# Longer packets, fewer fillers and earlier ranks at the head of an attention and mixture-of-experts kernel

## The chip, the cores and the metric

The kernel runs on one core of a Trainium2 chip. The metric is the device time of one execution in microseconds, the median of several runs.

## The reference

Linear attention is followed by two layers that send each token to one of eight experts. Cut to what matters:

```python
kv = np.einsum('bhsd,bhse->bhde', k, v)            # 4 batches, 8 heads, 576 rows, 64 wide
out = np.einsum('bhsd,bhde->bhse', q, kv)
x = out / np.sqrt(np.mean(out * out, -1, keepdims=True) + 1e-06) * g_norm   # to 2304 x 512

# first layer: a token with x @ w_skip > 0 goes to its best expert, the others stay as they are
e_idx = np.argmax(xc @ w_gate, axis=1)
h = np.maximum(xc[mask] @ w1[e], 0.0)               # 512 -> 1024
y[mask] = gate_w[mask, None] * (h @ w2[e])          # 1024 -> 512
out[do_compute] = xc + y

# second layer: every token, at most `capacity` per expert (576), the rest get 0
out[i] = gate_w[i] * y[expert_idx[i], pos[i]]
```

All of it is in 32-bit floating point. The order of k's and v's rows inside a batch does not change their product's sum.

## The kernel before

The kernel has three parts in one program. In the **attention part** the 2304 tokens are 18 tiles of 128 rows (`emit_tile`, L843). For each of the four batches `load_kv` (L737) and `load_q` (L753) bring k, v and q from the SyncE queue, `emit_kv` (L765) adds up the product of k and v in five steps c0 to c4 (four chunks of 128 rows and a rest of 64), and `emit_kvT` (L785) copies and transposes it and multiplies it by the gate weights. `emit_products` (L809) multiplies q by it for one tile into a bank pool of three (`apo`). ScalarE squares the tile and copies it out, VectorE takes the mean, its inverse and the logits (L850 to L863), GpSimd multiplies the copy by the gain and by the inverse (`multiply`, L827), and the rows are stored into a table in HBM, `xcat`, from the SyncE queue (L947).

TensorE's order is written out by hand. `ATT_SEQ` (L35) has one string for each batch: tN is a tile of that batch, mN its products alone, gN its gain, pN the rest of it, cN a step of the next batch's kv, T the end of that kv, r and R the two halves of `rank_part1` (L214), e and E the head of the first slot (`early1`, L871, and `early1_rows`, L878), f a run of fillers, w one load of the first slot's weights, q the transposes of its rows, h its first hidden step, s stores. The other engines' orders follow from these and from priorities.

`rank_part1` finds for the tokens seen so far which expert takes them and at what position. It runs once over tiles 0 to 8 and once over tiles 9 to 17. The first run also names the expert with most tokens; that expert's first 128 tokens are the first slot, and they are gathered from `xcat` and worked on while the attention part still runs. `As` (L271) and `Bt` are the two sides of the table of tokens, which TensorE multiplies (L883, L963). `EARLY_SEQ` (L34) is the order after the last tile: hidden steps h1 to h3, the second ranks R, output chunks y0 to y3, and T, the table.

A **filler** is a matrix product of zeros (`warm`, L109) that nothing reads. `WARM_0` (L36) has the number after each kv step of batch 0, `WARM_T` that in `emit_kvT`, `WARM_E` that of f.

In the **first layer** eight slots (one for each expert, by size) are worked in order (L1284 to L1317): two products, the tokens' new logits, and `add_tokens` (L995), which adds the slot's tokens to the table of the second layer in steps (`todo`). In slot 6 `early` (L1158) names the first expert of the second layer, gathers its rows and starts its weights. The **second layer** works its slots in the same way with every operand split in two halves. Weight buffers (`wr`) are a ring of six of 1 MB, used for k and v first.

## Time and profile before

| | us |
|---|---|
| median of three runs | 484.43 (483.7 to 484.61) |
| the profiled execution | 485.83 |
| its span, first to last instruction | 484.1 |
| TensorE busy in it | 470.4 |
| VectorE busy | 298.8 |
| ScalarE busy | 203.6 |
| GpSimd busy | 145.3 |

The profile is of one execution; times in it count from the start of its span. A row of the timeline has the start, the length, the engine, the line, the operation with what it writes and reads, how many instructions stand together, and in brackets how long the engine was idle before and what ended that. PE is TensorE, PEld its weight loads, DVE VectorE, ACT ScalarE, POOL GpSimd, SP SyncE. A matrix product in 32 bits counts as two instructions. A busy TensorE may be busy with fillers.

### The profile page before, as it was taken

How to read it: one execution, taken by the hardware profiler on the slowest of the kernel's cores; microseconds unless marked ns; L12 is line 12 of the kernel's file. 1: busy time of each engine (PE TensorE's matmuls, PEld its weight loads, DVE VectorE, ACT ScalarE, POOL GpSimd, SP SyncE). 2: the span in 40 equal slices, each digit the busy share in tenths (PEclk: the TensorE clock that was granted, in tenths of full speed). 3: DMA queues.
4: the chain of work that ended last, by engine and by line, in shares of the span. 5: the costliest groups of instructions: out<-in, count | busy, mean ns of one | idle time of the engine just before them, and what ended most of it. 6: DMA issues, size and time to landing. Idle time of an engine off the chain costs nothing.

```text
span 484.1 us, 10279 instructions
## 1 busy us (share of the span) xinstructions
PE 470.4 (97%) x3852; PEld 444.6 (92%) x3852; DVE 298.8 (62%) x950; ACT 203.6 (42%) x507; POOL 145.3 (30%) x179
## 2 busy tenths in 40 slices
PE   8999989999999999999899999999999999999995
PEld 3788788999999999999798999999999999999985
DVE  2367786676676755448694664756747656776611
ACT  1575542545353331225142553554545544555400
POOL 5586865022213113111243220401506033040201
PEclk9999999999999999999999999999999999999999
DMA  7999967997876955566039964554755566310001
GB/s 264 396 395 351 326 227 256 323 367 288 289 238 219 329 195 195 173 231 247 24 94 413 391 259 168 201 189 129 248 176 191 185 229 213 110 38 1 36 24 40
DMA packets 23641, 104.90 MB, mean 217 GB/s; under 512 B 3529, under 2 KB 3657, under 8 KB 14880
## 3 DMA queue, kind: packets, MB, share of 16 engines
q1 hardware_dynamic: 16144, 76.70, 44.6%
q0 software_dynamic: 7152, 27.40, 16.2%
q8 instruction: 32, 0.52, 0.4%
q14 instruction: 25, 0.20, 0.1%
q10 hardware_dynamic: 288, 0.07, 0.1%
HBM read 92.15 MB, written 12.76 MB: 217 GB/s over the span
## 4 chain that ended last, share of the span: by engine, by line
PE 74%; DVE 5%; DMA 3%; issue 1%; ACT 0%; POOL 0%; POOLq 0%; ACTq 0%
PE hp L677 13%; PE yp L1197 8%; PE yp L1198 8%; PE yp L1199 8%; PE hp L1197 6%; PE yp L701 6%; PE hp L1198 6%; PE hp L1199 6%; PE yp L711 3%; PE yp L702 2%; PE yt L1426 2%; PE tp L1382 2%; DMA wraw<-in_w2b 1%; DVE wlo L1087 1%; PE tp L659 1%; PE tp L1118 1%
## 5 line engine op out<-in xcount | busy, mean ns | idle before, releaser
L1086 ACT CAST whi<-wraw 128x512 fp32r<-128x512 f32 x152 | 86.3, 621 | 75.2 <-PE yp L1198 30.1
L1087 DVE TENSOR_TENSOR wlo<-wraw,whi 128x512 fp32r<-128x512 f32 x152 | 97.4, 684 | 28.9 <-ACT whi L1086 27.7
L416 POOL DMA_INDIRECT rows<-xcat,gi x40 | 42.6, 1064 | 149.0 <-ACT ex L425 87.8
L1197 PE MATMUL hp<-xh,whi 128*128 128x256 f32 (+7 forms) x256 | 78.9, 308 | 0.3 <-DVE hl L1217 0.2
L1199 PE MATMUL hp<-xh,wlo 128*128 128x256 f32 (+7 forms) x256 | 76.7, 299 | 0.0
L1198 PE MATMUL hp<-xl,whi 128*128 128x256 f32 (+7 forms) x256 | 76.6, 299 | 0.0
L677 PE MATMUL hp<-xT,wraw 128*128 128x140 f32 (+8 forms) x560 | 75.6, 291 | 0.5 <-ACT xT L661 0.5
L677 PEld LDWEIGHTS hp<-xT,wraw 128*128 128x128 f32 x560 | 71.6, 190 | 2.6 <-issue 1.8
L1197 PE MATMUL yp<-hh,whi 128*128 128x320 f32 (+5 forms) x192 | 58.8, 306 | 0.0
L1416 POOL DMA_INDIRECT out<-ot,toki x24 | 32.9, 1372 | 83.3 <-DVE su L429 39.5
L1198 PE MATMUL yp<-hl,whi 128*128 128x320 f32 (+5 forms) x192 | 57.3, 298 | 0.0
L1199 PE MATMUL yp<-hh,wlo 128*128 128x320 f32 (+5 forms) x192 | 57.3, 298 | 0.0
L1197 PEld LDWEIGHTS hp<-xh,whi 128*128 128x128 f32 x256 | 48.2, 188 | 1.0 <-DVE hl L1217 0.7
L1198 PEld LDWEIGHTS hp<-xl,whi 128*128 128x128 f32 x256 | 48.4, 189 | 0.0
L1199 PEld LDWEIGHTS hp<-xh,wlo 128*128 128x128 f32 x256 | 48.3, 189 | 0.0
L701 PE MATMUL yp<-hT,whi 128*128 128x352 f32 (+4 forms) x160 | 43.1, 351 | 0.0
L1136 POOL DMA_INDIRECT xcat<-rows,toki x16 | 17.0, 1062 | 82.4 <-DVE mxt L374 79.9
L1216 ACT ACTIVATE hh<-hp 128x320 fp32r<-128x320 f32 (+8 forms) x64 | 27.2, 430 | 32.2 <-PE hp L1199 27.4
L1217 DVE SCALAR_TENSOR_TENSOR hl<-hp,hh 128x320 fp32r<-128x320 f32 (+8 forms) x64 | 30.1, 477 | 13.7 <-ACT hh L1216 12.5
L702 PE MATMUL yp<-hT,wlo 128*128 128x176 f32 (+4 forms) x160 | 37.8, 236 | 0.0
L1198 PEld LDWEIGHTS yp<-hl,whi 128*128 128x128 f32 x192 | 36.2, 189 | 0.0
L1197 PEld LDWEIGHTS yp<-hh,whi 128*128 128x128 f32 x192 | 36.1, 188 | 0.0
(284 smaller groups left out, 854.2 us busy)
## 6 DMA issues: line engine op xcount, KB each, us to landing
wraw<-in_w2a SPq DMA_DIRECT2D x14, 1024.0 KB, 6.6
wraw<-in_w1b SPq DMA_DIRECT2D x14, 1024.0 KB
wraw<-in_w2b SPq DMA_DIRECT2D x14, 1024.0 KB, 5.2
wraw<-in_w1a SPq DMA_DIRECT2D x13, 1024.0 KB
xcat<-xa SPq DMA_DIRECT2D x18, 264.0 KB, 5.2
q<-in_q SPq DMA_DIRECT2D x4, 1152.0 KB
wraw<-in_k SPq DMA_DIRECT2D x6, 512.0 KB, 9.6
wraw<-in_v SPq DMA_DIRECT2D x6, 512.0 KB
```

What stands on the lines that cost most here:

```text
L416: return nc.gpsimd.indirect_dma_start(out=rows[:n], out_offset=None, in_=xcat[0:source], in_offset=bass.IndirectOffsetOnAxis(ap=gi[:n], ax ...
L677: nc.tensor.matmul(hp[:, ff, :], lhsT=wv[:, fc % 4, k, :], rhs=XT[j][:, k, c0:c1], start=(k == 0), stop=(k == 3))
L701: nc.tensor.matmul(yp, lhsT=wh[:, fc, :], rhs=HT[j][:, fc], start=(fc == 0), stop=False, skip_group_check=True)
L702: nc.tensor.matmul(yp[:, 0, :], lhsT=wl[:, fc, :], rhs=HT[j][:, fc, 0, :], start=False, stop=(fc == 7), skip_group_check=True)
L1086: nc.scalar.copy(out=hi[:, cs], in_=raw[:, cs])
L1087: ins = nc.vector.tensor_tensor(out=lo[:, cs], in0=raw[:, cs], in1=hi[:, cs].bitcast(F32), op=ALU.subtract)
L1197: nc.tensor.matmul(ps, lhsT=wh, rhs=xh, start=first, stop=False)
L1198: nc.tensor.matmul(ps, lhsT=wh, rhs=xl, start=False, stop=False)
L1199: nc.tensor.matmul(ps, lhsT=wl, rhs=xh, start=False, stop=last)
L1216: ea = nc.scalar.activation(out=hh[:, fs, cs], in_=hp, func=AF.Relu)
L1217: ev = nc.vector.scalar_tensor_tensor(out=hl[:, fs, cs], in0=hp, scalar=0.0, in1=hh[:, fs, cs].bitcast(F32), op0=ALU.max, op1=ALU.subtract)
L1416: st = nc.gpsimd.indirect_dma_start(out=out, out_offset=bass.IndirectOffsetOnAxis(ap=r2["toki"][:nn, j, bi:bi + 1], axis=0), in_=ot[:nn], ...
```

## The change

- k and v of a batch are loaded in two halves of two chunks, and each partition takes rows that follow one another, so that two chunks of a partition are one run of 4 KB. Batch 0 did it in four single chunks.
- There are 14 fillers at the start instead of 10, 3 instead of 15 between the kv steps of batch 0, 6 instead of 12 at f.
- The capacity is read into one partition; the overflow branch, where all 128 are wanted, reads it again.
- The first ranks stand ahead of tile 9, compare against the row of numbers in SBUF, and leave `bump` and `head` for after the table (`lead1_bump`). Tiles 9 and 10 have their products and copies early and the rest after the table; the gain is multiplied later.
- The kv of batch 3 lives in a bank of the tiles' pool, the transpose of batch 2's kv too.
- q of batch 3 is loaded after the stores of batch 1.
- The first slot's weights: the first half comes from GpSimd's queue after the gather, the other three from ScalarE's.
- VectorE multiplies tiles 12 and 14 by the gain straight from PSUM, instead of a copy by ScalarE and a product by GpSimd.
- The third hidden step of the first slot is cut in two around the second ranks, and the two bank pools there change places.
- In slot 6 of the first layer the third output chunk goes ahead of the last steps of the table, and `bump` is added after the fourth.

The core of the diff:

```diff
-G_DVE = ()
-EARLY_SEQ = "h1 x h2 R h3 y0 T y1 y2 y3"
-ATT_SEQ = ["t0 c0 c1 t1 t2 c2 c3 c4 t3 T s", "t0 t1 t2 c0 c1 t3 t4 c2 c3 c4 T s", "r c0 c1 t0 R e m1 g1 s9 w c2 c3 c4 m2 T E f p1 p2 t3", "t0 t1 s10 w s11 q t2 h0 t3 t4 s14 w s r"]
-WARM_0 = (5, 3, 5, 2, 0)
+G_DVE = (12, 14)
+EARLY_SEQ = "h1 x h2 a3 R b3 y0 T y1 y2 y3"
+ATT_SEQ = ["t0 c0 c1 t1 t2 c2 c3 c4 t3 T s", "t0 t1 t2 c0 c1 t3 t4 c2 c3 c4 T s l", "r c0 c1 R m0 g0 e m1 g1 c2 c3 c4 E T f p0 p1 w w w t2 t3", "t0 t1 s9 s10 q t2 h0 t3 s12 t4 s r"]
+WARM_0 = (0, 3, 0, 0, 0)
-WARM_E = 12
+WARM_E = 6
...
-    cap_i = cst.tile([128, 2], I32, name="cap_i")
-    nc.scalar.dma_start(out=cap_i, in_=capacity.bitcast(I32).unsqueeze(0).to_broadcast([128, 2]))
-    capf = cst.tile([128, 1], F32, name="capf")
+    cap_i = cst.tile([1, 2], I32, name="cap_i")
+    nc.scalar.dma_start(out=cap_i, in_=capacity.bitcast(I32).unsqueeze(0))
+    capf = cst.tile([1, 1], F32, name="capf")
...
-            nc.tensor.matmul(lg[:, 256:384], lhsT=ones[0:1], rhs=rowb[0:1], start=True, stop=True)
...
-            ahead["first"] = nc.vector.tensor_scalar(out=As[:, i0 + i, :], in0=row, scalar1=a[:, i:i + 1], scalar2=None, op0=ALU.is_equal)
+            ahead["first"] = nc.vector.tensor_scalar(out=As[:, i0 + i, :], in0=rowb, scalar1=a[:, i:i + 1], scalar2=None, op0=ALU.is_equal)
...
-        warm(p1u.tile([128, 512], F32, name="acc"), 10)
+        warm(p1u.tile([128, 512], F32, name="acc"), 14)
...
-            step = 1 if b == 0 else 2
-            for c in range(0, 4, step):
+            for c in range(0, 4, 2):
-                    nc.sync.dma_start(out=t[:, c:c + step, :], in_=src[b, o:o + 512].rearrange("(c p) d -> p c d", c=4)[:, c:c + step, :])
+                    nc.sync.dma_start(out=t[:, c:c + 2, :], in_=src[b, o:o + 512].rearrange("(p c) d -> p c d", c=4)[:, c:c + 2, :])
...
-            load_q(b)
+            if b < B - 1:
+                load_q(b)
...
+                if b == B - 1:
+                    spare.append(apo.tile([128, 4, 256], F32, name="ops").rearrange("p c n -> p (c n)"))
+                    kvp[b] = spare[-1][:, 0:512].rearrange("p (c n) -> p c n", c=4)
...
             if i in G_DVE:
                 nc.vector.tensor_tensor(out=og4, in0=o4, in1=grep.unsqueeze(1).unsqueeze(1).to_broadcast([128, 4, 2, HD]), op=ALU.mult)
-            else:
+                return
+            if i not in gained:
                 nc.scalar.copy(out=og4, in_=o4)
+            gained.add(i)
+            if whole:
                 multiply(og, og, grep.unsqueeze(1))
...
-                W[0].append(load_w(w1a, 1, nc.values_load(r1["lead"][0][0:1, 0:1], engines=[mybir.EngineType.Pool], min_val=0, max_val=E - 1,
-                                                          skip_runtime_bounds_check_because="the index of an expert"), nc.gpsimd, g))
+                W[0].append(load_w(w1a, 0, nc.values_load(r1["lead"][0][0:1, 0:1], engines=[mybir.EngineType.Pool], min_val=0, max_val=E - 1,
+                                                          skip_runtime_bounds_check_because="the index of an expert"), nc.gpsimd, g, ahead))
...
-                        W[0].append(load_w(w, hf, ahead["reg"], nc.sync, ahead["store"]))
+                        W[0].append(load_w(w, hf, ahead["reg"], nc.scalar))
...
             l2(j, 1)
+            if j == E - 2:
+                l2(j, 2)
             next(todo)
...
-            l2(j, 2)
+            if j != E - 2:
+                l2(j, 2)
+            l2(j, 3)
             if j == E - 2:
                 add(cnt2, identb, bump)
-            l2(j, 3)
```

## Rows read from the trace of the kernel before

**Rows 1.** The page: busy time and share, granted clock in forty slices.

```profile
PE 470.4 (97%) x3852; PEld 444.6 (92%) x3852; DVE 298.8 (62%) x950; ACT 203.6 (42%) x507; POOL 145.3 (30%) x179
...
PEclk9999999999999999999999999999999999999999
```

**Rows 2.** Waits of TensorE, 0 to 130 us: total, times, longest.

```profile
PE lg L241 <- DVE oh L167: 1.3, 1, 1.3
```

**Rows 3.** Timeline of TensorE, from the start into batch 1.

```profile
1.48 4.23 PE L112 MATMUL acc<-zb 128*128 128x512 bf16 x10 [1.48 <-DVE zb L107]
...
8.36 0.69 PE L777 MATMUL acc<-wraw 128*64 128x64 f32 x16 [0.28 <-DMA wraw<-in_v]
...
10.35 1.25 PE L112 MATMUL lg<-zb 128*128 128x512 bf16 x5
...
12.69 0.68 PE L777 MATMUL acc<-k,v 64*64 64x64 f32 x16
...
17.94 1.15 PE L777 MATMUL acc<-wraw 128*64 128x64 f32 x32
```

**Rows 4.** Timeline around the first ranks and the first gather.

```profile
39.20 0.24 DVE L159 TENSOR_REDUCE lg<-xa 128x9 f32<-128x72 f32 x1 [1.76 <-ACT kvbd L804]
...
46.79 1.10 DVE L271 TENSOR_SCALAR As<-lg,a 128x128 bf16<-128x128 f32 x4
...
48.38 2.75 PE L112 MATMUL ops<-zb 128*128 128x512 bf16 x12 [0.24 <-ACT kvbd L804]
...
49.80 1.28 POOL L416 DMA_INDIRECT rows<-xcat,gi  x1 [4.24 <-DMA xcat<-xa]
```

**Rows 5.** VectorE's groups, 40 to 66 us: count, busy us, mean ns, idle before.

```profile
L850 DVE TENSOR_REDUCE ss<-sq 128x8 f32<-128x512 f32 x9 | 6.0, 677 | 3.8 <-ACT sq L848 3.8
L863 DVE TENSOR_REDUCE xa<-lh 128x17 f32<-128x136 f32 x9 | 3.3, 377 | 0.1
...
L861 DVE TENSOR_TENSOR lh<-ops,ri 128x136 f32<-128x136 f32 x9 | 2.6, 292 | 0.2
L858 DVE RECIPROCAL ri<-rm 128x8 f32<-128x8 f32 x9 | 1.8, 199 | 0.1
L934 DVE COPY xT<-lg 128x512 f32<-128x512 f32 x1 | 0.7, 681 | 0.0
```

**Rows 6.** DMA queues: packets, MB; first row 0 to 7 us, second 3.9 to 5.9.

```profile
q1 hardware_dynamic: 545, 1.01, 52.6%
...
q10 hardware_dynamic: 114, 0.00, 2.7%
```

**Rows 7.** Stretches: length, busy time of each engine, granted clock, DMA share, GB/s.

```profile
3.90:5.90 2.00, 1.81 (x5) 0.45 (x3) 0.59 (x3) 0.00 (x0) 0.00 (x0) 1.00 0.60 94
6.00:10.00 4.00, 3.51 (x48) 2.04 (x50) 2.39 (x14) 0.00 (x0) 2.33 (x9) 1.00 1.04 395
11.00:13.40 2.40, 2.40 (x38) 1.41 (x37) 0.00 (x0) 0.00 (x0) 1.86 (x10) 1.00 1.04 431
```

**Rows 8.** Timeline from the first hidden step to the end of the second ranks.

```profile
57.67 1.95 PE L677 MATMUL lg<-xT,wraw 128*128 128x128 f32 x16
...
66.73 0.42 PE L241 MATMUL lg<-oh,ones 128*128 128x72 bf16 x9 [1.33 <-DVE oh L167]
...
70.07 1.21 DVE L271 TENSOR_SCALAR As<-rowb,a 128x128 bf16<-128x128 bf16 x7
```

**Rows 9.** Timeline: a load issued from ScalarE's queue.

```profile
1.37 0.39 ACTq L119 DMA_DIRECT2D cap_i<-in_capacity  x1
```

**Rows 10.** Timeline around the first slot of the second layer.

```profile
212.60 1.02 POOL L416 DMA_INDIRECT rows<-xcat,gi  x1 [0.31 <-issue]
...
221.59 1.04 PE L1209 MATMUL tp<-ident,rows 128*128 128x128 f32 x8
...
231.05 0.57 PE L986 MATMUL acc<-Bo,A 128*128 128x16 bf16 x6 [0.80 <-DVE A L1021]
```

**Rows 11.** Stretches, columns as in rows 7, after TensorE's last instruction.

```profile
480.00:482.00 2.00, 0.00 (x0) 0.00 (x0) 0.00 (x0) 0.00 (x0) 0.29 (x1) 1.00 0.35 101
```

More of the change, by code (lines that the diff above doesn't have):

```diff
@@ L306, in lead1_rest @@
         nc.vector.scalar_tensor_tensor(out=head, in0=oneP, scalar=8192.0, in1=sev, op0=ALU.mult, op1=ALU.add)
[L307 removed]
+        st["head"] = head
+        return bump
     def run(gen):
@@ L408, in load_w @@
             behind(ins, after)
+        if note is not None:
+            note["gather"] = ins
         return t
```

74 lines of the change are left out of this document (45 added, 29 removed).

## The prediction

> **What bounds the kernel now.** I read the page first. TensorE is busy for 97% of the span and its granted clock stands at full speed in every slice [rows 1], so a change can only pay by taking work out of TensorE's own order or by closing a hole in it. Next I read who TensorE waited for up to 130 us: the longest wait for data is the 1.3 us for the one-hots of the second ranks [rows 2]. Busy is not useful, though. A filler (L112) computes nothing, and the timeline of TensorE shows them standing where the engine would otherwise wait: ten at the start, then 5, 3, 5 and 2 between the five steps of batch 0's k and v [rows 3], and twelve at 48.38 [rows 4]. So the third view is that of the stretches, for what stands behind the fillers. At the start that is the loads. At 48.38 it is VectorE, which builds the first ranks while TensorE has no free bank. After 50 us it is VectorE again, which needs 0.677 + 0.199 + 0.292 + 0.377 = 1.55 us for each tile [rows 5]. From 77 us on TensorE is closed but for small gaps, so what is gained before it should come out whole at the end.
>
> **The start.** Twelve fillers go between the steps of batch 0 (15 become 3), four are added ahead of them, and k and v arrive in two pairs of chunks each rather than four single chunks. After its last wait for a load, at 8.36, TensorE goes by its own order up to the fifth step at 12.69 [rows 3]; fillers are in that order, so now the loads decide. The fifth step needs 2.62 MB. The queue had moved 1.01 MB by 7.0 us [rows 6] and moves 395 GB/s after that [rows 7], so the bytes are there at 7.0 + 1.61 / 0.395 = 11.1 us. Three things move this.
> - The capacity is read into one partition rather than 128. From 3.9 to 5.9 us the loads fall to 94 GB/s [rows 7], just while 114 packets of the other queue pass with next to no bytes [rows 6]. I put the hole down to those packets: 2.0 x (1 - 94/395) = 1.5 us earlier. From below it is worth 0, if the hole has another cause.
> - A row of two chunks is 4 KB in one packet instead of two of 2 KB. The trace has no 4 KB rows. Its nearest are 395 GB/s where 2 KB rows run and 431 where q's 9 KB rows run [rows 7]; with a fixed time for a packet and one for a byte 4 KB gives 415, so the 2.1 MB concerned take 0.26 us less. The ends are 0 and 0.45 us.
> - From bytes to landing: the second step needs 1.05 MB, there by about 7.1 us, and began at 8.36 [rows 3], so a load may be seen up to 1.3 us after its mean byte.
>
> The fifth step can begin at 11.1 - 1.5 - 0.26 = 9.3, plus 0 to 1.3. TensorE's own order allows 9.7: fourteen fillers up to about 6.6 (ten took 4.23 us [rows 3], four more at 0.22), four steps of 0.62 and three fillers. So it begins at 9.7 to 10.6 instead of 12.69: 2.1 to 3.0 us. What is late next is batch 1: q of batch 0 (1.18 MB at 431) and the first pair of chunks (1.05 MB at 415) end at 9.3 + 2.7 + 2.5 = 14.6, plus 0 to 1.3, and TensorE wants them at 17.94 - 2.4 = 15.5 [rows 3], which may cost up to 0.4. I take **2.2 us**, and for the bounds 0.6 (hole not closed) and 3.0.
>
> Here a rule speaks against the change. The Trainium skill (DMA: Bandwidth & Descriptors, Specifications) has line rate from 512 B per transfer on, by which longer rows would bring nothing and the start 1.9 us rather than 2.2. The two stretches differ by 9%, so this trace does not agree.
>
> **The first ranks.** They are put ahead of tile 9, and the transpose of batch 2's kv uses another bank. Before, VectorE began the ranks 1.76 us late because their bank still held that transpose [rows 4]; then it did tile 9 between their steps (1.55 us), and compared nine tiles against a row in PSUM, 0.26 us each where they follow closely (the last four, 1.10 us) [rows 4]; the second ranks, which compare against bf16 in SBUF, need 1.21 / 7 = 0.17 [rows 8]. So the tables end 1.76 + 1.55 + 9 x 0.09 = 4.1 us earlier by VectorE; TensorE's kv steps of batch 3, now ahead of the table, hold it to some 3.2 us. The gather stood at 49.80 and waited for the stores of tiles 0 to 8 [rows 4]. Those now go ahead of q of batch 3 in SyncE's queue, 1.18 MB / 431 = 2.7 us earlier, besides the 1.8 us of the start, so the gather can follow. That q now waits for store 8 to be issued, with only later stores queued behind it; it still lands some 2.5 us before tile 13 wants it, so I cost this at nothing.
>
> The twelve fillers at 48.38 become six. That is no gain by itself: tile 11 needs the spare bank, which is free when batch 3's kv has been copied. That is only some 0.6 us sooner than before, and tile 11, which used to be done before the fillers, now comes after them. I work tile 12 out to start 2.0 us sooner than 51.19.
>
> **The late tiles.** From the gather on VectorE has nine tiles (before: eight), and the two products with the gain. Nothing shows such a product from PSUM; the nearest row copies 128x512 from PSUM in 0.68 us [rows 5], the ends are 0.5 and 1.0. Together 9 x 1.55 + 2 x 0.68 + 0.68 for the transposed rows = 16.0 us after the first ranks end, at about 46.2 on the old scale: 62.2 without any idle. Before, the last tile's logits were ready at 64.8, the start of the ranks at 66.73 less their 1.9 us. Walking tile by tile I find some idle time and get 63 to 64.1. So the second ranks begin 0.7 to 1.8 us earlier, and 0 if VectorE falls back further. I take **1.0 us**. GpSimd loses two products and ScalarE two copies; neither decides here, and this cover is gone only if the last store becomes late for the gathers after the ranks.
>
> The weights of the first slot: three issues move to ScalarE, 0.39 us each by the one shown [rows 9], and a read of the slot's expert, ready some 3 us before; the activations of tiles 11 and 12 are queued behind them. VectorE is the slower engine there, so 0, at most 1.0 us. SyncE's stores no longer share a queue with them. The weights that the first layer needs first come from GpSimd behind the gather; even at half of 395 GB/s, 1 MB takes 5.3 us, about when TensorE turns to them (57.67 before [rows 8], some 1.5 earlier now).
>
> Half of the third hidden step goes ahead of the second ranks and half behind. It fills 1.0 of the 1.33 us of waiting at 66.73 [rows 8], but the table of the second ranks still waits for VectorE's As, 4.5 us after the ranks begin, and TensorE comes to it 1 us sooner: the gap moves. 0, at most 0.3.
>
> **The second layer's first slot.** In slot 6 the third output chunk moves ahead of the tables, so the head of the second MoE is known 2 us later, and with it the gathers (second issue 212.60) and the first load. The transposes at 221.59 need those rows, and the 0.80 us that TensorE waits at 231.05 comes from a VectorE queue that has two splits more to fit in [rows 10]. I take **-0.3**; the ends are +0.2 and -1.3. The reading of the capacity inside the overflow branch costs nothing here, since the branch isn't taken.
>
> Sum: 2.2 + 1.0 - 0.3 = 2.9 us. Against the profiled execution (485.83, span 484.1) that is 482.9; it ran 1.4 us above the median of the three runs, and against that median the time is 484.43 - 2.9 = **481.5 us**.
>
> **Rivals.**
> - *The late tiles give nothing.* With 1.36 us more on VectorE and a copy of the first slot's rows queued behind it, hidden step 0 delays tiles 16 and 17 and the second ranks stand where they did. For it: VectorE's 16.0 us. Against: the tables are 3 us early. 484.43 - 2.2 + 0.3 = 482.5.
> - *The hole isn't the capacity's.* Then the start gives 0.6 to 1.9, say 1.3: 484.43 - 1.3 - 1.0 + 0.3 = 482.4. With both of these, 483.4.
> - *More than I took:* start 3.0, ranks 1.7, slot 6 nothing: 479.7.
> - *Slower: TensorE's clock falls.* With twelve fillers gone TensorE stands idle between the pairs of chunks. At the lower level the first ten fillers took 0.42 us each, against 0.22 later [rows 3], and they took 4.2 us before the level rose. A fall that lasts as long costs half of it, 2.1 us; two cost 4.2: 484.43 - 2.9 + 4.2 = 485.7. It decides from 5.8 us at 1.2 GHz on. Against it: the gaps that I expect are below 1 us, the wait of 1.33 us left the clock alone, and at 480 to 482 us it is still at full speed with TensorE idle [rows 11].
>
> The Trainium skill (TensorE: Matmul & The Clock Gate, HAM oscillation) describes short bursts with waits for loads between them that put the clock back again and again, which is this rival. No row of this trace shows such a fall, which is why it gets little.
>
> **Numbers.** My forecast 0.52, no gain from the late tiles 0.18, hole stays 0.12, more 0.09, clock 0.09. The range from 479.5 to 484.0 takes in the second, third and fourth and leaves out the clock and sums of several bad ends. About 0.2%, 1 us, is what a measurement of this kernel tells from no change; faster needs under 483.5. From the cases: faster 0.80 (the forecast, more, and most of the two partial gains), same 0.11, slower 0.09.
>
> **What would show it.** The loads at 350 GB/s or more from 4 to 6 us, and the fifth kv step at 9.7 to 10.6; the gather about 5.4 us earlier than 49.80; tile 12 about 4 us earlier than 51.19; the second ranks at 63 to 64; every later step 3 us earlier; at 231 us a wait like the old one. It is wrong if matmuls of one shape take longer before 20 us (clock), if hidden step 0 waits, or if the gap before the first matmuls of the second MoE grows by over 1 us.

## The result, and the profile after

The changed kernel is slower: 488.51 us (485.79 to 489.19, six runs) against 484.27 beside it, a ratio of 1.0078 (95% interval 1.0050 to 1.0107). Run again later beside the experiments it gave 488.71 us and 1.0062 (1.0040 to 1.0084). The forecast was 481.5, range 479.5 to 484.0, chance of slower 0.09. All comparisons below are such ratios to the kernel before, from runs on the same chip, since its own median moved between 483.8 and 485.2 from one set to the next. Four executions that lie far above the others of their kernel (933 us of the kernel before, and 578, 493 and 935 us among the experiments) are left out of the ratios.

| | before, us | after, us |
|---|---|---|
| the profiled execution | 485.83 | 488.28 |
| its span | 484.1 | 486.6 |
| TensorE busy | 470.4 | 466.6 |
| VectorE busy | 298.8 | 298.1 |
| ScalarE busy | 203.6 | 201.3 |
| GpSimd busy | 145.3 | 144.1 |

TensorE is busy for 3.8 us less (the fillers are gone) and the span is 2.5 us longer, so over 6 us of waiting came in. Who TensorE waited for in the kernel after: engine, what it was to write and on which line, whom it waited for, us in total, times, longest.

```profile
PE acc L796 <- DMA wraw<-in_v: 2.6, 3, 1.5
PE ops L842 <- DVE lh L883: 1.7, 2, 1.1
PE lg L690 <- DVE xT L958: 1.6, 1, 1.6
PE tp L1412 <- DMA rows<-xcat,gi: 1.5, 1, 1.5
...
PE tp L1236 <- DMA rows<-xcat,gi: 1.1, 1, 1.1
```

In the old list the longest wait behind the start was the 1.3 us for the one-hots [rows 2]; that wait fell to 0.4. In its place stand three loads of k and v (L796), VectorE's logits of a tile (L842), VectorE's copy of the first slot's transposed rows (L690), and gathered rows twice (L1236, L1412). Taken in order of time:

**The start.** TensorE's timeline, answering [rows 3]:

```profile
7.49 1.15 PE L796 MATMUL acc<-wraw 128*64 128x64 f32 x32 [0.41 <-DMA wraw<-in_v]
10.08 1.15 PE L796 MATMUL acc<-wraw 128*64 128x64 f32 x32 [0.68 <-DMA wraw<-in_v]
11.39 0.68 PE L796 MATMUL acc<-k,v 64*64 64x64 f32 x16 [0.16 <-DMA v<-in_v]
...
18.10 1.15 PE L796 MATMUL acc<-wraw 128*64 128x64 f32 x32 [1.51 <-DMA wraw<-in_v]
```

The fifth step is at 11.39 instead of 12.69, but the first step of batch 1 at 18.10 instead of 17.94: it waits 1.51 us for its load. 1.3 us were won and all of it is lost seven microseconds later. The stretches (the last two columns are the DMA share and GB/s) answer [rows 7]:

```profile
3.90:5.90 2.00, 2.00 (x6) 0.76 (x5) 0.00 (x0) 0.00 (x0) 0.00 (x0) 1.00 0.93 238
6.00:10.00 4.00, 2.99 (x39) 1.50 (x37) 2.94 (x17) 0.00 (x0) 2.39 (x9) 1.00 1.01 399
14.00:16.00 2.00, 2.00 (x14) 1.44 (x14) 0.00 (x0) 0.86 (x2) 0.00 (x0) 1.00 1.02 406
```

The hole from 3.9 to 5.9 is half filled, 238 GB/s where there were 94.

**The late tiles.** The table of the first ranks is at 44.12 and the gather at 45.88, 3.9 us earlier than 49.80 [rows 4], where about 5.4 were forecast. Then the timeline of TensorE, answering [rows 8]:

```profile
48.03 4.23 PE L842 MATMUL ops<-kvbd,q 128*128 128x162 f32 x32
53.36 1.34 PE L842 MATMUL ops<-kvbd,q 128*128 128x162 f32 x8 [1.10 <-DVE lh L883]
54.54 0.60 PE L957 MATMUL lg<-ident,rows 128*128 128x128 f32 x4
55.72 1.34 PE L842 MATMUL ops<-kvbd,q 128*128 128x162 f32 x8 [0.58 <-DVE lh L883]
58.69 2.05 PE L690 MATMUL lg<-xT,wraw 128*128 128x128 f32 x16 [1.64 <-DVE xT L958]
...
67.85 0.40 PE L240 MATMUL lg<-oh,ones 128*128 128x72 bf16 x9 [0.43 <-DVE oh L167]
```

The first row holds tiles 11 to 13 (the last of them, across two batches, takes two sets of products), so tile 12 is 2.1 us earlier than 51.19. Three waits of 3.3 us in all follow, and hidden step 0 (58.69) is 1.0 us later than before, the second ranks (67.85) 1.1 us. ScalarE and VectorE in that stretch:

```profile
49.83 0.58 ACT L861 COPY xa<-ops 128x512 f32<-128x512 f32 x1
50.11 0.38 ACTq L411 DMA_DIRECT2D wraw<-in_w1a  x1
50.74 1.42 ACTq L411 DMA_DIRECT2D wraw<-in_w2a  x2
52.21 0.30 ACT L878 ACTIVATE rm<-ss,eps 128x8 f32<-128x8 f32 x1 [1.80 <-issue]
...
52.61 0.20 DVE L880 RECIPROCAL ri<-rm 128x8 f32<-128x8 f32 x1 [1.96 <-ACT rm L878]
...
57.29 0.68 DVE L858 TENSOR_TENSOR xa<-ops,au 128x512 f32<-128x512 f32 x1
57.89 0.19 DVE L880 RECIPROCAL ri<-rm 128x8 f32<-128x8 f32 x1
58.00 0.64 DVE L958 COPY xT<-lg 128x512 f32<-128x512 f32 x1
```

ScalarE issues three loads from 50.11 to 52.16 and does tile 11's root only then; VectorE stands idle for 1.96 us and is late from there on. The first slot's rows are transposed by 55.1, and VectorE copies them at 58.00, behind a tile's whole chain and a product with the gain.

**Slot 6 and after.** TensorE, answering [rows 10]:

```profile
222.81 0.27 PE L1236 MATMUL tp<-ident,rows 128*128 128x128 f32 x1
224.16 0.99 PE L1236 MATMUL tp<-ident,rows 128*128 128x128 f32 x7 [1.07 <-DMA rows<-xcat,gi]
...
232.61 0.30 PE L1013 MATMUL acc<-Bo,A 128*128 128x16 bf16 x6
...
234.71 0.39 PE L1224 MATMUL hp<-xh,whi 128*128 128x256 f32 x1
...
257.97 0.33 PE L1412 MATMUL tp<-ident,rows 128*128 128x128 f32 x1 [1.50 <-DMA rows<-xcat,gi]
```

The wait at 231 is gone and one of 1.07 us at 224 has come, since the gathers are issued 3.1 us later (second issue 215.72 against 212.60). The first product of the second layer is at 234.71 against 233.42 in the trace of before. At 258 a later gather costs another 1.5 us.

### The profile page after: what moved, and what is told of

The parts are those of the page before. It is cut to its first block, busy times and chain, and to the rows that moved or that the text cites. A ratio compares the mean times of both kernels' runs of the same rounds, so it can differ in the third digit from the quotient of the medians.

```text
span 486.6 us, 10236 instructions
## 1 busy us (share of the span) xinstructions
PE 466.6 (96%) x3833; PEld 443.7 (91%) x3837; DVE 298.1 (61%) x952; ACT 201.3 (41%) x505; POOL 144.1 (30%) x177
## 4 chain that ended last, share of the span: by engine, by line
PE 72%; DMA 5%; DVE 4%; issue 1%; ACT 1%; POOL 0%; POOLq 0%; ACTq 0%
PE hp L690 10%; PE yp L1224 7%; PE yp L1226 7%; PE yp L1225 7%; PE hp L1224 7%; PE hp L1226 7%; PE hp L1225 7%; PE yp L716 6%; PE yp L726 5%; PE yp L717 2%; DMA wraw<-in_w2a 2%; PE tp L1412 2%; DMA wraw<-in_w1b 2%; DMA rows<-xcat,gi 2%; PE yt L1456 2%; PE tp L1145 1%
## 5 line engine op out<-in xcount | busy, mean ns | idle before, releaser
L690 PE MATMUL hp<-xT,wraw 128*128 128x140 f32 (+8 forms) x560 | 75.7, 291 | 0.2 <-ACT xT L672 0.2
L690 PEld LDWEIGHTS hp<-xT,wraw 128*128 128x128 f32 x560 | 71.6, 190 | 2.3 <-issue 1.8
L1446 POOL DMA_INDIRECT out<-ot,toki x24 | 34.7, 1445 | 85.4 <-DVE su L436 39.9
L1244 DVE SCALAR_TENSOR_TENSOR hl<-hp,hh 128x320 fp32r<-128x320 f32 (+8 forms) x64 | 30.1, 476 | 15.4 <-ACT hh L1243 15.2
```

Of the source, the lines that this page charges most:

```text
L690: nc.tensor.matmul(hp[:, ff, :], lhsT=wv[:, fc % 4, k, :], rhs=XT[j][:, k, c0:c1], start=(k == 0), stop=(k == 3))
L1244: ev = nc.vector.scalar_tensor_tensor(out=hl[:, fs, cs], in0=hp, scalar=0.0, in1=hh[:, fs, cs].bitcast(F32), op0=ALU.max, op1=ALU.subtract)
L1446: st = nc.gpsimd.indirect_dma_start(out=out, out_offset=bass.IndirectOffsetOnAxis(ap=r2["toki"][:nn, j, bi:bi + 1], axis=0), in_=ot[:nn], ...
```

## The experiments

My theory after reading the two traces: three losses at three places, namely ScalarE's issues and VectorE's queue at the late tiles, the order of slot 6, and a start that gives nothing after 18 us. The rivals: each of these only moves a wait. The first four experiments undo one part each in the kernel after. Where an experiment has an expectation, "the theory" and "the rival" behind it are the two that it names.

### Slot 6 in its old order

```diff
-            if j == E - 2:
-                l2(j, 2)
             next(todo)
...
-            if j != E - 2:
-                l2(j, 2)
-            l2(j, 3)
+            l2(j, 2)
             if j == E - 2:
                 add(cnt2, identb, bump)
+            l2(j, 3)
```

> The kernel after the change, with slot 6 of the first layer in its old order (third output chunk behind the table steps, the bump added ahead of the fourth chunk). Theory: the later head of the second MoE (gathers at 214.36 and 215.72 in the kernel after, 211.23 and 212.60 before) costs the 1.1 us wait for gathered rows at 224 and starts everything of the second layer late, and with the later gathers the 1.5 us wait of the t2 transposes at 258. Undone, the gathers are 3 us earlier, the wait at 224 is gone, the 0.8 us wait at 231 is back, and the time is 1.3 to 2.8 us less than the kernel after: 485.7 to 487.2. Rival: the wait only changes its place (0.8 at 231 instead of 1.1 at 224) and the time is within 0.5 us of the kernel after, 488.0 to 489.0, with the loss elsewhere.

Measured: 487.1 us, ratio 1.0041 (1.0022 to 1.0060), that is 0.2 to 0.4% less than the kernel after. In its trace the gathers are at 211.77, the wait at 224 is gone, and none stands at 231. From the transposes at 204 to the first product of the second layer it takes 28.84 us, against 30.13 in the kernel after. The 1.2 us wait for rows at 256 stayed. So the reorder costs 1.3 us; the rival falls.

### The loads on SyncE's queue, early

```diff
-ahead["reg"] = nc.values_load(..., engines=[mybir.EngineType.Activation], ...)
+ahead["reg"] = nc.values_load(..., engines=[mybir.EngineType.SP], ...)
-W[0].append(load_w(w, hf, ahead["reg"], nc.scalar))
+W[0].append(load_w(w, hf, ahead["reg"], nc.sync))
```

> The kernel after the change, with the three weight loads of the first slot issued from SyncE's queue instead of ScalarE's, at the same place of the order. Theory: the three issues hold ScalarE for 2 us (50.1 to 52.2), so the root of tile 11 comes late, and with it VectorE (idle 1.96 us there), tile 14, the transposed rows and hidden step 0. Without them VectorE has no idle time at 52.6, hidden step 0 waits under 0.3 us instead of 1.64, the second ranks begin 1.0 to 1.5 us earlier than 67.85, and the time is 1.0 to 1.5 us less than the kernel after: 487.0 to 487.5. Rival: VectorE's own queue (nine tiles, two products with the gain, the copy of the transposed rows) sets the place of hidden step 0 whoever issues the loads: ranks at 67.5 to 67.9, 488.3 to 488.7.

Measured: 489.9 us, 1.0091 (1.0067 to 1.0115): neither came. ScalarE had no stall and tile 14 waited only 0.57 us, but SyncE issued the three loads from 44.10 to 45.8, ahead of GpSimd's load of the first half, which then landed last. TensorE's timeline:

```profile
54.43 1.27 PE L842 MATMUL ops<-kvbd,q 128*128 128x162 f32 x8
59.95 3.14 PE L690 MATMUL lg<-xT,wraw 128*128 128x128 f32 x16 [4.26 <-DMA wraw<-in_w1a]
```

And the stretch from 60 to 64 (busy time of PE, PEld, DVE, ACT and POOL, then granted clock, DMA share, GB/s):

```profile
60.00:64.00 4.00, 4.00 (x21) 4.00 (x22) 0.20 (x1) 0.57 (x2) 0.00 (x0) 0.58 0.45 167
```

It is also the one trace with the prediction's clock rival: after 4.26 us without work the granted clock (third column from the right) is 0.58 from 60 to 64, so for most of it at the lower of its two levels, 1.2 instead of 2.4 GHz, and the 16 products take 3.14 us instead of 2.05. In the kernel after, with waits up to 1.64 us, the clock stood at 1.00 there.

### No products with the gain on VectorE

```diff
-G_DVE = (12, 14)
+G_DVE = ()
```

> The kernel after the change, with tiles 12 and 14 multiplied by the gain as all the others are (copied by ScalarE, multiplied by GpSimd). Theory: on VectorE the two products are 0.68 us each and one stands straight ahead of the copy of the transposed rows; without them that copy comes 0.7 us earlier, hidden step 0 waits 0.9 instead of 1.64 us, the second ranks begin 0.7 to 1.4 us earlier than 67.85 and the time is 0.7 to 1.4 us less than the kernel after: 487.1 to 487.8. Rival: VectorE was waiting for ScalarE anyway at 52.6 and takes the products in that time; then the ranks stay at 67.5 to 67.9 and the time at 488.3 to 488.7.

Measured: 486.45 us, 1.0022 (1.0006 to 1.0038). Hidden step 0 waits 0.81 us, the second ranks begin at 66.38, 1.47 us earlier than in the kernel after, and the time is 0.4 to 0.6% less than that of the kernel after: the theory, with a little more than it expected.

### The old start

```diff
-WARM_0 = (0, 3, 0, 0, 0)
+WARM_0 = (5, 3, 5, 2, 0)
-        warm(p1u.tile([128, 512], F32, name="acc"), 14)
+        warm(p1u.tile([128, 512], F32, name="acc"), 10)
...
-            for c in range(0, 4, 2):
+            for c in range(0, 4, step):
...
-                    nc.sync.dma_start(out=t[:, c:c + 2, :], in_=src[b, o:o + 512].rearrange("(p c) d -> p c d", c=4)[:, c:c + 2, :])
+                    nc.sync.dma_start(out=t[:, c:c + step, :], in_=src[b, o:o + 512].rearrange("(c p) d -> p c d", c=4)[:, c:c + step, :])
...
-    nc.scalar.dma_start(out=cap_i, in_=capacity.bitcast(I32).unsqueeze(0))
+    nc.scalar.dma_start(out=cap_i, in_=capacity.bitcast(I32).unsqueeze(0).to_broadcast([128, 2]))
```

> The kernel after the change, with the start as it was before: batch 0 of k and v in four single chunks with rows of 2 KB, two chunks of 2 KB rows for the other batches, ten fillers and then 5, 3, 5 and 2, the capacity read into 128 partitions. Theory: the start gave 1.3 us up to 15.2 us and nothing from 18.1 us on, since the last of the 16 DMA engines has the first pair of batch 1 no sooner (one is held up by an instruction fetch of 1.07 us at 14 us). Undone, the step of batch 1 stands at 17.7 to 18.1 and the time is that of the kernel after within 0.5 us: 488.0 to 489.0. Rival (the prediction's term of 2.2 us): the time is 1.3 to 2.2 us more, 489.8 to 490.7.

Measured: 487.23 us, 1.0030 (1.0006 to 1.0053), if anything below the kernel after (by 0.3 to 0.5%), not above it; the first step of batch 1 at 17.68. The new start is worth nothing or a little less, and my term of 2.2 us is refuted.

### The loads on SyncE's queue, between the late stores

```diff
-... E T f p0 p1 w w w t2 t3", "t0 t1 s9 s10 q t2 h0 t3 s12 t4 s r"]
+... E T f p0 p1 t2 t3", "t0 t1 s9 w s10 w q t2 h0 t3 s12 w t4 s r"]
```

(and the engine as above)

> The kernel after the change, with the three weight loads of the first slot issued from SyncE's queue between the stores of the late tiles (after stores 9, 10 and 12), not from ScalarE's and not ahead of the gather. Theory: ScalarE no longer stands for 2 us, and the loads no longer run ahead of the first half from GpSimd's queue, as they did when SyncE issued them at 44 us. Tile 14 waits under 0.6 us instead of 1.1, the transposed rows are copied 0.5 to 1.2 us sooner, hidden step 0 begins at 57.4 to 58.2 instead of 58.69 and the second ranks at 66.5 to 67.3 instead of 67.85: 0.5 to 1.4 us less than the kernel after. Rival: VectorE's two products with the gain hold the place: ranks at 67.5 to 67.9 and no difference to the kernel after within 0.4 us.

Measured: 483.91 us, 0.9984 (0.9959 to 1.0009): 0.6 to 0.9% less than the kernel after. The loss is gone, and against the kernel before no difference clears the noise. TensorE:

```profile
52.88 1.34 PE L842 MATMUL ops<-kvbd,q 128*128 128x162 f32 x8 [0.57 <-DVE ri L880]
54.06 0.60 PE L957 MATMUL lg<-ident,rows 128*128 128x128 f32 x4
54.50 1.27 PE L842 MATMUL ops<-kvbd,q 128*128 128x162 f32 x8
55.61 1.95 PE L690 MATMUL lg<-xT,wraw 128*128 128x128 f32 x16
...
64.66 0.40 PE L240 MATMUL lg<-oh,ones 128*128 128x72 bf16 x9 [0.44 <-DVE oh L167]
```

The second ranks are 3.2 us earlier than in the kernel after and 2.1 earlier than before, more than I expected. The edit had moved more than it names. A planner in the framework sets the order of each engine's queue from priorities and from the times that it estimates; with other times to plan by, the order of VectorE's queue came out differently too, and the copy of the transposed rows now ran at 54.70, ahead of tile 14's product with the gain. That question needed a run of its own (the last one).

### All three undone

> The kernel after the change with three things undone at once: weight loads on SyncE's queue between the late stores, no product with the gain on VectorE, slot 6 in its old order. Theory: the three costs are at different places and add up: second ranks at 65.0 to 66.0 (66.38 with the gain alone undone, 66.73 before), 1.2 us less between 204 and 233, no late rows at 258: 1.5 to 2.8 us faster than the kernel before, 482.4 to 483.7 beside a before of 485.2. Rival: the loss comes with the earlier ranks themselves (nine tiles on VectorE after the table) and stays: second ranks at 66.4 or later, and no faster than the kernel before within 0.8 us.

(the edits above: loads between the stores, `G_DVE = ()`, slot 6 as before)

Measured: 484.29 us, 0.9997 (0.9973 to 1.0021). The time is the rival's, though the place is not: the ranks begin at 64.19, earlier than even the theory had them, and slot 6 has its 28.84 us, but the three gains don't add up. The second ranks' table waits, and the timeline of VectorE, GpSimd and TensorE shows what stands beside that wait:

```profile
65.67 0.62 DVE L345 TENSOR_TENSOR EQ<-rowf,slot 128x64 f32<-128x64 f32 x1
66.32 0.96 DVE L329 TENSOR_TENSOR oe<-EQ,rowf 1x64 f32<-1x64 f32 x1
...
65.17 2.04 POOL L849 TENSOR_TENSOR xa<-xa,ri 128x512 f32<-128x512 f32 x2
...
68.53 1.33 PE L990 MATMUL acc<-Bt,As 128*128 128x32 bf16 x9 [1.01 <-DVE Bt L210]
```

The same two VectorE rows where the loads alone were moved (the kernel of the section before):

```profile
66.05 0.22 DVE L345 TENSOR_TENSOR EQ<-rowf,slot 128x64 f32<-128x64 f32 x1
66.31 0.21 DVE L329 TENSOR_TENSOR oe<-EQ,rowf 1x64 f32<-1x64 f32 x1
```

With two products more, GpSimd works until 67.2 (until 65.0 in the other), and two small VectorE operations that lie in that time take 0.62 and 0.96 us instead of 0.22 and 0.21. Each ends 0.07 to 0.08 us after the GpSimd product beside it; in the 16 other traces no GpSimd product lies beside these two rows, and they take 0.20 to 0.22 us. So, once ScalarE is out of the way, the products with the gain on VectorE cost 0.5 us at the ranks (64.66 against 64.19), and moving them to GpSimd gives up 1.0 us right behind the ranks. That the whole time is no better than in the section before is not explained any further: TensorE waits 1.29 us for rows at 253, but in the kernel of the section before it waits 1.27 us at 254.

### Slot 6's new order alone, in the kernel before

> The kernel before, with the new order of slot 6 alone. Theory: the wait at 231 (0.80 us before) goes and one of 1.0 us for the gathered rows comes at 222, so the first product of the second MoE keeps its place within 0.4 us (233.0 to 233.8, 233.42 before) and the time its own within 0.1%. Rival, from the order undone in the kernel after (28.84 us from the transposes at 204 to the first product of the second MoE, against 30.13): the old order without its wait is 1.2 us shorter, so the new one costs 0.5 to 1.2 us here as well.

Measured: 486.8 us, 1.0057 (1.0024 to 1.0090): the rival. From 204.64 to the first product of the second layer at 234.76 it takes 30.12 us.

### The new start alone, in the kernel before

(with the new reading of the capacity in the overflow branch)

> The kernel before, with the new start alone: rows of 4 KB, two pairs of chunks, fourteen fillers and three later, the capacity read into one partition. Theory: 1.0 to 1.3 us earlier up to the products of batch 0 (15.2 instead of 16.5) and nothing from batch 1 on: its first step at 17.8 to 18.2 (17.94 before), the time within 0.1% of the kernel before. Rival (the prediction's term): 1.3 to 2.2 us faster.

Measured: 484.97 us, 1.0019 (0.9997 to 1.0042). The fifth step is at 11.58, the first of batch 1 at 18.12: the theory. This run also settles what was odd about slot 6. It has the old order, and 28.83 us there, without a wait at 231; the trace of before needed 30.07. ScalarE in the trace of before:

```profile
224.25 0.62 ACT L1190 CAST whi<-wraw 128x512 fp32r<-128x512 f32 x1 [1.25 <-DMA wraw<-in_w2b]
```

The same instruction in this kernel's trace:

```profile
223.14 0.62 ACT L1193 CAST whi<-wraw 128x512 fp32r<-128x512 f32 x1
```

In the execution that was profiled before the change, a load of weights came 1.1 us late; ScalarE waited for it with the copy of the transposed rows queued behind, VectorE was late from that, and TensorE waited at 231 [rows 10]. In the seven other traces with the old order, this one among them, the wait isn't there and the stage takes 28.83 or 28.84 us. The wait that I meant to weigh was an accident of one execution, and with 1.24 us it explains most of the 1.4 us by which that execution lay above the median.

### The loads late and slot 6 old, the products kept

> The kernel after the change, with the weight loads of the first slot on SyncE's queue between the late stores and slot 6 in its old order; the two products with the gain stay on VectorE. Theory: second ranks at 64.5 to 64.8 as with the loads alone moved (64.66), no wait for the ranks' table, 28.8 us instead of 30.1 from the transposes at 201 to the first product of the second MoE: 229.5 to 230.1 there (233.42 before) and 2.0 to 3.5 us faster than the kernel before, ratio 0.993 to 0.996. Rival: what is won before 230 is given back at the rows of the second layer's next slot (wait of 1.2 to 1.6 us at 252), ratio 0.997 to 0.999.

Measured: 484.39 us, 0.9978 (0.9959 to 0.9997), the lowest ratio of all, though within the noise of two others (0.9984 and, below, 0.9981). It is well under the kernel after, but against the kernel before the gain is only 0.0 to 0.4%, which is less than the theory expected and lies in the rival's range. The places are as forecast (ranks 64.55, first product of the second layer 229.94, span 480.6 in the profiled execution); that execution was the fastest of twelve, and the others lie up to 3.3 us above it. The three slowest (485.4 to 485.7 us) have a mean granted clock of 0.993 to 0.994, the others 0.996 to 0.999. The wait that the rival names is not in the profiled execution, and the slower ones left no trace.

### The kernel after, again

> The kernel after the change, unaltered, beside the others on the same chip: 0.4 to 1.0% slower than the kernel before, with the wait of 1.6 us of hidden step 0 for the transposed rows.

Measured: as told above, 1.0062 (1.0040 to 1.0084), with the same 1.64 us at hidden step 0.

### The same with the old start

> As the kernel with the loads moved and slot 6 in its old order, and with the start of the kernel before (2 KB rows, single chunks for batch 0, all fillers, the capacity in 128 partitions). Theory: the start gives nothing after 18 us, so the time is within 0.5 us of that kernel, and the kv step of batch 1 within 0.4 us of its place there. Rival: 1 to 2 us slower than that kernel.

Measured: 484.35 us, 0.9981 (0.9958 to 1.0003), no difference; batch 1's first step at 17.68 against 18.04. So the start, taken alone, added to the kernel after and added to the best one, makes the time 0.2, 0.3 to 0.5 and 0.0% longer (each uncertain by about 0.3): nothing is won.

### The capacity in 128 partitions

```diff
-    nc.scalar.dma_start(out=cap_i, in_=capacity.bitcast(I32).unsqueeze(0))
+    nc.scalar.dma_start(out=cap_i, in_=capacity.bitcast(I32).unsqueeze(0).to_broadcast([128, 2]))
```

> The kernel after the change, with the capacity read into 128 partitions again, everything else of the start as in the kernel after. If the 114 small packets make the hole of the loads, the bytes from 3.9 to 5.9 us fall from 238 to about 70 to 100 GB/s, the first pair of chunks comes 0.5 to 1 us later than 7.5 and the fifth step 0.5 to 1.5 us later than 11.4. If the hole comes from the short rows or from the start of the queue itself, they stay at 200 to 240 GB/s and the fifth step at 11.2 to 11.9.

A single execution, to read its trace. The stretches of this kernel:

```profile
3.90:5.90 2.00, 2.00 (x7) 0.74 (x6) 0.00 (x0) 0.00 (x0) 0.00 (x0) 1.00 0.84 219
6.00:7.00 1.00, 0.67 (x4) 0.10 (x1) 0.59 (x3) 0.00 (x0) 0.00 (x0) 1.00 0.75 222
```

The same stretches of the kernel after with the whole old start:

```profile
3.90:5.90 2.00, 2.00 (x5) 0.45 (x3) 0.59 (x3) 0.00 (x0) 0.00 (x0) 1.00 0.69 66
6.00:7.00 1.00, 0.90 (x17) 0.87 (x18) 0.84 (x7) 0.00 (x0) 0.10 (x1) 1.00 1.03 399
```

With the 114 packets back and the rows long, the hole of 3.9 to 5.9 does not come back; a smaller one appears from 6 to 7, where the kernel after had 377 GB/s, and the fifth step is at 12.12, 0.2 to 0.7 us later than with the narrow read (11.39 to 11.91 in the kernels with the new start). So the packets cost 0.2 to 0.7 us here, not 1.5, as far as one execution tells. The deep hole goes with the shape of the first loads: the traces with single chunks of 2 KB rows and the wide read have 66 to 105 GB/s there, long rows with the wide read 219, long rows with the narrow read 217 to 238. No run has single chunks with the narrow read, so whether the short rows would make the hole without the 114 packets stays open.

### Long rows with the old fillers

(the kernel with the loads late and slot 6 old; `WARM_0` and the ten fillers as before, the loads as after)

> The kernel after the change, with the weight loads on SyncE's queue between the late stores, slot 6 in its old order, and the fillers of the start as before (10, then 5, 3, 5 and 2); the long rows and the single capacity stay. Theory: with fewer fillers TensorE comes sooner to the place where the 16 KB instruction packet is fetched (14.5 to 15.5 us in the four kernels with the new start, 19 to 20 in the four with the old one), and that packet holds one of the 16 DMA engines while the first pair of batch 1 is on its way (last engine at 17.9 to 18.2, median 16.3 to 17.0). With the old fillers the packet is at 19 us or later, the pair has landed by 17.3 and its first step begins at 17.4 to 17.7 instead of 18.04: 0.3 to 0.6 us less than with the new fillers. Rival: long rows land late by themselves (spread of the 16 engines over 1.5 us also without the packet): 17.9 to 18.2 as there.

Measured: 484.8 us, 0.9991 (0.9964 to 1.0019). A list from the raw trace, one line for each of ten kernels: when the 16 KB packet of the queue of kind "instruction" starts (it takes 1.06 to 1.09 us), when the last of the 16 DMA engines has the first pair of batch 1, how far first and last are apart, and when TensorE's first step of batch 1 begins, in us.

```
kernel                          packet   last engine   spread   step
before                          20.2     17.81         1.00     17.94
after, old start                20.1     17.55         0.58     17.68
before, slot 6 new              19.5     17.30         0.38     17.43
best, old start                 20.1     17.49         0.70     17.68
before, loads on ScalarE        19.6     17.26         0.59     17.39
after                           15.0     17.96         1.96     18.10
before, new start               15.2     17.99         1.92     18.12
best (loads late, slot 6 old)   15.3     17.90         1.75     18.04
after, capacity wide            15.6     18.23         1.75     18.37
best, old fillers               19.3     16.91         0.76     19.05
```

With the new start the packet comes 4 to 5 us earlier, while that pair is on its way, and one DMA engine falls a microsecond behind the others; the load counts as landed with the last of them. Seven more traces with the new start, not in the list, agree (packet at 15.2 to 15.5, last engine at 17.9 to 18.0). Only the fillers differ between the last line and the eighth: the packet is back at 19.3 and the pair is there a microsecond sooner. So the theory holds for the load (that it is the packet and not something else that comes with fewer fillers rests on the two moving together in all 17 traces), and the rival (long rows are late by themselves) falls. The step itself came at 19.05, not at 17.4 to 17.7 as I expected: the first pair of batch 0 came only at 7.79, and with 15 fillers in TensorE's order behind it the engine is busy until then. What makes the packet move (TensorE, with eight fillers less in its stream, runs ahead) is only argued.

That a load is there when its last engine is there is also what the Trainium skill says (DMA: Bandwidth & Descriptors, Why a DMA increments its semaphore by 16 and not by 1: the engines finish independently and only the full count means all data); the steps above start 0.13 to 0.19 us after the last engine in every line but the last, so the trace agrees.

### The three loads on ScalarE, one at a time, in the kernel before

```diff
-W[0].append(load_w(w, hf, ahead["reg"], nc.sync, ahead["store"]))
+W[0].append(load_w(w, hf, ahead["reg"], nc.scalar))
```

> The kernel before, with its three weight loads of the first slot issued by ScalarE at the places where SyncE issued them, one at a time between the late tiles. Theory: what cost 3 us in the kernel after is that three issues stand together ahead of the root of one tile; one at a time each costs ScalarE 0.4 to 0.7 us, of which VectorE's queue feels little: second ranks at 66.6 to 67.5 (66.73 before), 0 to 0.8 us slower. Rival: an issue on ScalarE waits whenever its queue is full or its buffer late, whatever its place: second ranks at 68.5 or later, 2 to 4 us slower.

Measured: 486.0 us, 1.0007 (0.9977 to 1.0038). A tile waits 1.32 us for VectorE's logits instead of 0.34 for ScalarE; from tile 12 to the second ranks it takes 16.5 us (50.59 to 67.11) instead of 15.5. So three single issues, with the reading of the slot's number that goes to ScalarE with them, cost 1.0 us together in that stretch, and there the rival falls. The whole time shows no difference that clears the noise.

### Only the copy ahead, in the kernel after

```diff
-nc.vector.tensor_copy(out=XT[0][:, :, 0:128], ...)
+with tc.high_priority():
+    ahead["xt"] = nc.vector.tensor_copy(out=XT[0][:, :, 0:128], ...)
+behind(ahead["ri13"], ahead["xt"])
+behind(ahead["g14"], ahead["xt"])
+behind(ahead["ss14"], ahead["xt"])
```

> The kernel after the change, with the three loads left on ScalarE, and only the copy of the first slot's transposed rows put ahead on VectorE: ahead of tile 13's inverse, tile 14's mean and tile 14's product with the gain, where it stands when the loads are moved (in the kernel after it stands behind them all, at 58.00 us, though the rows are transposed by 55.1). Theory: of the 3.2 us by which the second ranks came sooner with the loads moved, the stall of ScalarE itself is 0.5 to 1.2 and the place of the copy the rest; so here hidden step 0 begins at 56.4 to 57.0 instead of 58.69 and the second ranks at 65.5 to 66.3 instead of 67.85, 1.5 to 2.4 us less than the kernel after. Rival: the stall is the whole cause, since VectorE has as much to do in either order: ranks at 67.3 or later, and no gain over 0.5 us.

Measured: 484.86 us, 1.0004 (0.9980 to 1.0029), 0.6 to 0.7% less than the kernel after. VectorE, then TensorE:

```profile
55.71 0.68 DVE L960 COPY xT<-lg 128x512 f32<-128x512 f32 x1
...
56.70 1.95 PE L690 MATMUL lg<-xT,wraw 128*128 128x128 f32 x16
...
65.75 0.40 PE L240 MATMUL lg<-oh,ones 128*128 128x72 bf16 x9 [0.43 <-DVE oh L167]
```

ScalarE still stalls (its root of tile 11 is at 52.01), and yet the ranks begin at 65.75. Of the 3.2 us between 67.85 and 64.66 the place of one copy of 0.68 us on VectorE makes 2.1; the other 1.1, what is left, goes to ScalarE's stall.

## Why the prediction was wrong

Four steps failed: the start, whose hole was put down to the 114 packets and whose 2.2 us were taken as won; VectorE's late work, summed without the order of its queue; ScalarE's three issues, taken at 0; and slot 6, where a wait of one execution was set against the delay.

| term | forecast | what the runs showed |
|---|---|---|
| start | 2.2 us faster (0.6 to 3.0) | 0 or less: first step of batch 1 at 18.0 to 18.2 (17.4 to 17.9 with the old start); what that costs is already in the ranks of the next row |
| first ranks and late tiles, copy in time | 1.0 faster (0 to 1.8) | 2.1 faster at the second ranks, with the loads moved |
| place of the copy on VectorE | in a rival, at 0 | 2.1 slower |
| three loads issued by ScalarE | 0 (at most 1.0 slower) | 1.1 slower |
| slot 6 | 0.3 slower (+0.2 to -1.3) | 1.3 slower |

The right column makes 2.4 us slower, 0.5%; the two measurements were 0.6 and 0.8%, 3.0 and 3.8 us. What is left, 0.6 to 1.4 us, I can't put to a part. There are two candidates, and no run isolates either.

The first is what stands behind the first product of the second layer. From there to TensorE's last product it takes 244.9 us in the trace of before, 245.8 in that of after, 247.5 in the second one of after and 244.8 in the best. TensorE waits for gathered rows at 250 to 258: 1.5 us in the trace of after, 0.6 in the second one, 0 in that of before, 0.9 in the kernel before with the new start, and 0 to 1.3 in the best two. A little later, at 263 to 265, it waits for VectorE: 0.2 us in the trace of after, 1.8 in the second one, 0 in that of before. Both waits change from execution to execution.

The second is TensorE's clock in executions that were not profiled. Of 18 executions of the kernel after, six have a mean granted clock of 0.993 to 0.995, like all six of the second experiment, whose trace shows a fall of the clock; their median is 489.5 us, that of the other twelve 487.9. Of the kernel before only 10 of 131 are as low. A fall in a third of the executions would raise the median of the kernel after by some 0.6 us (an estimate from these medians), but none of the six left a trace.

- **The bound.** That TensorE's order decides and that fillers stand where it would wait was right: each loss is a wait of TensorE, and 3.8 us less of work ended 2.5 us later. That a gain ahead of 77 us "should come out whole at the end" held only part of the way. In the profiled execution of the best kernel the second ranks are 2.18 us earlier than before and the transposes at 201 still 2.25 us earlier; behind the second layer's first product, waits that differ from one execution to the next can take as much. No rival on the list reached 488.5 (the slowest had 485.7), since several terms failed at once.
- **The start failed twice.** The fifth step came 1.3 us earlier instead of 2.1 to 3.0, and nothing of it was left at batch 1. The step "I put the hole down to those packets" gave 1.5 us; with long rows the packets cost 0.2 to 0.7. Then the step "a load may be seen up to 1.3 us after its mean byte" carried the landing of batch 1. The sums of bytes were not bad: by 16 us the kernel after has moved 5.01 MB, that of before 4.72. But the 4.85 MB up to the first pair (all of batch 0, 3.8, and 1.05) are there at 15.6 and the step begins at 18.10, 2.5 us later. I had looked for the gap between bytes and landing at one early place and not asked what else passes through the 16 engines. My own warning, that batch 1 may be late by 0.4, was the right place; 1.5 us were waited there.
- **The first ranks** came out as worked out: the frame gave 2.0 us for tile 12 and 2.1 were measured. That frame leaves out the start; with it "about 4" was forecast. The gather was 3.9 us earlier, not 5.4: the forecast had 2.2 us of the start in it and 3.2 without them, so the ranks gave a little more than was worked out and the start nothing.
- **The late tiles.** The price of the products was right (0.64 to 0.68 us, 0.68 taken), the sum of VectorE's work too: with the copy in time and the loads elsewhere the ranks begin 2.1 us earlier, above my 1.0. What failed is that I summed VectorE's queue and did not ask for the order in it. My first rival names the very mechanism, "a copy of the first slot's rows queued behind it, hidden step 0 delays tiles 16 and 17 and the second ranks stand where they did"; with 0.18 it got too little and its price of 0 left out that hidden step 0 could come later than before.
- **ScalarE's issues.** "VectorE is the slower engine there, so 0, at most 1.0": the issue was taken from one row of 0.39 us [rows 9], three are 1.2, and the stall was 2.1 us (two of them took 1.42 together, with the reading of the slot's number ahead). It put VectorE idle for 1.96 us, so VectorE was not the slower engine just then. The bound of 1.0 was nearly the 1.1 measured; the value taken was the wrong end.
- **Slot 6.** The sign was right, and the size stood at the far end of my range. I set the old wait of 0.80 against the delay and so expected to win part back. The wait was named as VectorE's in the trace, and one step further back it was a late load. A single execution was read as the rule.
- **The clock rival** did not happen in the two profiled executions of the kernel after, where the granted clock stands at 1.00 up to TensorE's last product. It did in the second experiment, behind 4.26 us of waiting: 16 products took 3.14 instead of 2.05 us and the next 16 took 2.94 instead of 2.37, 1.7 us for the fall against the 2.1 that the prediction priced it at. Whether it came in other executions of the kernel after is open, as said above.
- **What would show it** worked: all the places named (loads, fifth step, gather, tile 12, second ranks, hidden step 0, the gap before the second layer) differ from the forecast where the terms failed.

## What to carry to other kernels

Of a step in front of which an engine may stand idle, ask not how much that engine has to do but what stands ahead of it in the queue, and look it up again after each edit, since a planner may reorder another engine's queue. A DMA issue on a computing engine was paid here by whatever stood behind it: three in a row at the worst place cost 1.1 us, three single ones 1.0 in that stretch, and none of it was seen with the loads on SyncE's queue between the stores. Before a wait in one profile is put into a sum, see whether a second execution has it.

## What the runs showed of the hardware that was not expected

- One 16 KB packet of kind "instruction", 1.07 us long, holds one of the 16 DMA engines; the pair of loads behind it was complete 1.0 to 1.1 us later than without it (three kernels with long rows against one), though the median engine was not late (16.3 to 16.5 us with it, 16.4 without). With eight fillers less around it, it moved from 19.3 to 20.2 us to 15.0 to 15.6. That the packet is what holds that engine is inferred from the two moving together in all 17 traces.
- VectorE operations on 64 elements took 0.62 and 0.96 us instead of 0.22 and 0.21 while GpSimd multiplied, and reductions of 512 elements beside such products did not (0.69 in both). Both stretched ones read two tensors from SBUF. The Trainium skill (GPSIMD Engine Reference, Specifications) says that GpSimd's path to SBUF is shared with VectorE, with contention when VectorE's instructions run in a 2-port performance mode or have two SBUF inputs. The two rows agree. Two inputs are not needed, though: in the trace of after a copy with one input is stretched beside GpSimd's writing of zeros, and one of the same shape just ahead of it, beside another GpSimd operation, is not. It ends 0.03 us after the first of the two GpSimd instructions (8.48 us). No run shows which mode an operation ran in.

```profile
7.63 0.16 DVE L81 COPY pi<-pcol 128x18 f32<-128x18 f32 x1
7.88 1.17 POOL L743 MEMSET vk<- 128x512 f32 x2
7.94 0.57 DVE L82 COPY pi<-im 128x18 f32<-128x18 f32 x1
```

- After 4.26 us without a product TensorE ran at the lower level of its clock for most of 60 to 64 us, and 16 products took 3.14 us instead of 2.05. Waits of 1.0 to 1.9 us in the other traces (1.64 in that of after, 1.82 in that with the old start) left it at 1.00.
